# Gate and up projections as Strassen 2x2 block products, with attention as a phase of its own before the feed-forward

## The chip, the cores and the metric

The kernel runs on one core of one Trainium2 chip. The metric is the device time of one execution in microseconds (us). Three runs of the kernel before gave 1727.75, 1727.91 and 1728.28 us. Engines are named as in the profile: PE (matrix products), PEld (its weight loads), DVE (vector), ACT (scalar), POOL, and SP, whose queue issues the DMAs.

## The reference

One input `x` (2048 tokens by 576) goes through two branches which are mixed per token by a sigmoid gate:

```python
g = sigmoid((x * gate_w).sum(-1, keepdims=True))
# a: 32 heads of 18; q, k, v = x @ wqkv; pq = q @ w_phi, pk = k @ w_phi by head
phi = concat(softmax(p), softmax(-p))              # for pq and pk
kv  = phi_k^T v;  z = sum_s phi_k                  # over all tokens
a   = concat_heads(phi_q kv / (phi_q z + 1e-6)) @ wo
# b: gated feed-forward, 4608 hidden
b = (relu(x @ W_gate) * (x @ W_up)) @ W_down
return g * a + (1 - g) * b
```

Everything is float32. The sum over all tokens in `kv` must be finished before any query output can be made; the feed-forward needs nothing of attention.

## The kernel before

Every float32 operand is split into a rounded high part and the exact remainder (`split`: ACT writes `h`, then DVE writes `l = src - h`). A product of two split operands is three matmuls (high by high, low by high, high by low). A contraction of 576 is four tiles of 128 rows and a fifth tile that holds the last 64 rows twice, which needs two matmuls only: `products` yields 4 x 3 + 2 = 14 matmuls for a 128 x 512 result.

Work is tiled by 512 tokens (`TB`, four blocks `tb`) and by 128 hidden rows (36 chunks `c`); `units` holds all 144 pairs.

1. **Keys and values.** For each of 16 token tiles of 128: projections `pk`, `pv` (28 matmuls each of the two), `dual_softmax` (DVE row maxima and minima, two subtractions, ACT exponential, DVE sums, reciprocals) and `scale_heads`, then `kv_step` adds to five PSUM accumulators `kv`.
2. **Feed-forward with attention between its pieces.** For each unit, `gate_up(u, between)` makes the 14 `gate` matmuls, the 14 `up` matmuls, and the hidden rows (times 1 - g, split in `hh`, `hl`); `down(u - 1)` adds 14 matmuls to five PSUM accumulators `acc` that stay open for a whole token block. Between gate and up, `between()` advances the generator `attention(tb)` by one piece: a half projection `pq`, a group of four transposes `ptr`, one `po` product, or one of five output products, which add straight into `acc` (L443). So attention's PE work stands in small pieces between matmuls of the feed-forward, and its DVE and ACT work has a whole token block of 36 units to be done in.

The weights of a unit (928 KB: gate, up and down) are loaded and split again for each of the four token blocks, so 144 times. The order of instructions on each engine is set by a scheduler from the program's order and dependencies; each engine then works through its own list in order.

In the changed kernel (line numbers are its own) the steps that the prediction names are `queries`, `turn` and `outputs` (attention's three parts), `x_operands` and `operand` (the split operands of x), `split_blocks`, `split_sums`, `split_down` (a unit's weights), `product`, `down` and `finish`.

Of the kernel before, what the change touches and what calls it, by code (L numbers as in the profile page):

```python
# [7 lines left out]
F32 = mybir.dt.float32  # L8
# [6 lines left out]
DH = D // H  # L15
# [14 lines left out]
WB = 2 * DK + D  # L30
# [3 lines left out]
def gated_mix_kernel(  # L34
    ctx: ExitStack,
    tc: tile.TileContext,
    xT: bass.AP,
    wqT: bass.AP,
# [4 lines left out]
    wb: bass.AP,  # L43
# [4 lines left out]
    """Products in float32 run as float32r ones: each operand is split exactly into two parts of  # L48
    12 significant bits. A contraction of 576 is four tiles of 128 and a tile that holds the last
    64 rows twice, high parts above low parts."""  # L50
    nc = tc.nc
    PSUM = bass.MemoryType.PSUM

    keep = ctx.enter_context(tc.tile_pool(name="keep", bufs=1))
    raw = ctx.enter_context(tc.tile_pool(name="raw", bufs=2))
    xp = ctx.enter_context(tc.tile_pool(name="xp", bufs=2))
    wp = ctx.enter_context(tc.tile_pool(name="wp", bufs=3))
    hp = ctx.enter_context(tc.tile_pool(name="hp", bufs=2))
    soft = ctx.enter_context(tc.tile_pool(name="soft", bufs=2))
    pp = ctx.enter_context(tc.tile_pool(name="pp", bufs=3, space=PSUM))  # L60

    ident = keep.tile([P, P], F32, name="ident")
    mask = keep.tile([G, G], F32, name="mask")
    ones = keep.tile([1, P], F32, name="ones")
    gs = keep.tile([P, NT], F32, name="gs")
    wq_h = keep.tile([P, 5, D], F32R, name="wq_h")
    wq_l = keep.tile([P, 5, D], F32R, name="wq_l")
# [4 lines left out]
    def split(hi, lo, src):  # L72
        nc.scalar.activation(hi, src, AF.Copy)  # L73
        nc.vector.tensor_tensor(out=lo, in0=src, in1=hi.bitcast(F32), op=ALU.subtract)  # L74
# [8 lines left out]
    def split_x4(x4, src):  # L83
        nc.scalar.activation(x4, src, AF.Copy)
        nc.vector.tensor_tensor(out=x4[64:], in0=src[64:], in1=x4[64:].bitcast(F32), op=ALU.subtract)
# [12 lines left out]
    def products(wh, wl, x, xs=slice(0, TB)):  # L98
        xh, xl, x4 = x
        for k in range(4):  # L100
            yield wh(k), xh[:, k, xs]
            yield wl(k), xh[:, k, xs]
            yield wh(k), xl[:, k, xs]
        yield wh(4), x4[:, xs]
        yield wl(4), x4[:, xs]
# [12 lines left out]
    def dual_softmax(p):  # L118
        """exp(p - max p) and exp(min p - p) by head, and the reciprocals of their sums."""
# [5 lines left out]
        e = soft.tile([P, 2, D], F32, name="e")  # L125
        eh = e.rearrange("p s (h f) -> p s h f", f=DH)
        nc.vector.tensor_tensor(out=eh[:, 0], in0=ph, in1=mx[:, :, None].to_broadcast([P, H, DH]),
                                op=ALU.subtract)
        nc.vector.tensor_tensor(out=eh[:, 1], in0=mn[:, :, None].to_broadcast([P, H, DH]), in1=ph,
                                op=ALU.subtract)  # L130
        nc.scalar.activation(e, e, AF.Exp)
        sm = soft.tile([P, 2 * H], F32, name="sm")
        nc.vector.tensor_reduce(out=sm, in_=e.rearrange("p s (h f) -> p (s h) f", f=DH), axis=AX, op=ALU.add)
# [4 lines left out]
    def scale_heads(e, r):  # L138
        eh = e.rearrange("p s (h f) -> p (s h) f", f=DH)
        nc.vector.tensor_tensor(out=eh, in0=eh, in1=r[:, :, None].to_broadcast([P, 2 * H, DH]), op=ALU.mult)  # L140

# [1 line left out]
    units = [(tb, c) for tb in range(NTB) for c in range(NC)]  # L143
    RAW, W, HID, NGB = {}, {}, {}, {}

    def load_chunk(u):
        if u < len(units):
            RAW[u] = raw.tile([P, WB], F32, name="wbr", tag="raw")
            nc.sync.dma_start(RAW[u], wb[units[u][1]])

    def split_half(u, o):
        if u < len(units):
            h = wp.tile([P, DK], F32R, name="gh")
            l = wp.tile([P, DK], F32R, name="gl")
            split(h, l, RAW[u][:, o:o + DK])
            W[u, o] = h, l

    def split_rest(u):
        if u < len(units):
            split_half(u, DK)  # L160
            w = RAW.pop(u)[:, 2 * DK:]
            dh = wp.tile([P, DK], F32R, name="dh")
            dl = wp.tile([P, 512], F32R, name="dl")
            nc.scalar.activation(dh[:, :D], w, AF.Copy)
            nc.vector.tensor_tensor(out=dl, in0=w[:, :512], in1=dh[:, :512].bitcast(F32), op=ALU.subtract)
            nc.vector.tensor_tensor(out=dh[:, D:], in0=w[:, 512:], in1=dh[:, 512:D].bitcast(F32), op=ALU.subtract)
            W[u] = dh, dl

    def half(u, o, name):
        h, l = W.pop((u, o))  # L170
        ps = bank(name)
        accumulate(ps, products(lambda k: h[:, k * P:(k + 1) * P], lambda k: l[:, k * P:(k + 1) * P],
                                X[units[u][0]]))
        return ps

    def gate_up(u, between=lambda: None):
        """A chunk of hidden rows, times 1 - g. The weights of the next chunks are split meanwhile."""
        r = hp.tile([P, TB], F32, name="r", bufs=1)
        hh = hp.tile([P, TB], F32R, name="hh")
        hl = hp.tile([P, TB], F32R, name="hl")  # L180
        nc.scalar.activation(r, half(u, 0, "gate"), AF.Relu)
        split_rest(u + 1)
        between()
        nc.vector.tensor_tensor(out=r, in0=r, in1=half(u, DK, "up"), op=ALU.mult)  # L184
        nc.vector.tensor_tensor(out=r, in0=r, in1=NGB[units[u][0]], op=ALU.mult)  # L185
        split(hh, hl, r)
        split_half(u + 2, 0)
        HID[u] = hh, hl

    def gates(tb):  # L190
        """1 - g of a block's tokens, on every partition."""
        pg = bank("pg")
        for i in range(4):
            t = 4 * tb + i
            nc.tensor.transpose(pg[:, i * P:(i + 1) * P], gs[:, t:t + 1].to_broadcast([P, P]), ident)  # L195
        NGB[tb] = keep.tile([P, TB], F32, name="ngb", bufs=2)
        nc.scalar.activation(NGB[tb], pg, AF.Copy, bias=1.0, scale=-1.0)

# [12 lines left out]
    with tc.tile_pool(name="ps_v", bufs=1, space=PSUM) as ps_v:  # L211
        pv = [[(bank("pv") if n < 3 else ps_v.tile([P, TB], F32, name=f"pv{n}"))[:, :VC[n % 2][1]]
               for n in (2 * i, 2 * i + 1)] for i in range(4)]
        # TensorE's clock gate opens while the first loads arrive.
        warm = hp.tile([P, TB], F32R, name="hh")
# [82 lines left out]
    load_chunk(0)  # L298
    load_chunk(1)
    split_half(0, 0)  # L300
    split_rest(0)
    load_chunk(2)
    split_half(1, 0)
    fold(wqT, wq_h, wq_l)
    gates(0)
    gate_up(0)
# [3 lines left out]

# [1 line left out]
    a2 = ctx.enter_context(tc.tile_pool(name="a2", bufs=1))  # L312
    pt = ctx.enter_context(tc.tile_pool(name="pt", bufs=22))
    st = ctx.enter_context(tc.tile_pool(name="st", bufs=1))
    kt = [pt.tile([GS, 2, G], F32, name="kt", tag="pt") for _ in range(NG)]
    for j, (c0, gn) in enumerate(GROUPS):
# [234 lines left out]
```

## Time and profile before

| what | value |
|---|---|
| runs | 1727.75, 1727.91, 1728.28 us |
| profiled execution: span of its core | 1724.7 us (the median of the runs is 3.2 us above this span) |
| PE busy / matmuls | 1714.8 us / 8243 |
| DVE busy | 971.1 us |
| ACT busy | 669.2 us |
| granted PE clock | 0.998 on average |
| DMA | 170.33 MB, mean 99 GB/s |

The busy time of an engine is the time in which at least one of its instructions ran, so instructions that overlap their neighbours count once there, while the mean length of one instruction is its full length. Starts of consecutive matmuls are closer than one matmul is long, since they are pipelined. The chain of waits names, from the end backwards, what each step waited for. A few matmul records are missing from the trace.

### The profile page before, as it was taken

What the parts mean: (1) busy time and instruction counts of PE and PEld (TensorE: products, weight loads), DVE (VectorE), ACT (ScalarE), POOL (GpSimd) and SP (SyncE); (2) the same over time, 40 slices, a digit from 0 to 9 for tenths busy, and PEclk for the clock granted to TensorE, in tenths of its full rate; (3) what the DMA queues carried; (4) which work ended last, traced back from release to release, by engine and by line L of the source; (5) the groups of instructions that cost most, each with busy time, mean ns of one, the idle gap of its engine ahead of it and who ended that gap; (6) DMA issues with size and microseconds to landing.
All of it is one profiled execution on the core that took longest, in us unless ns stands there. A gap on an engine that the chain in (4) does not pass through costs nothing.

```text
span 1724.7 us, 20764 instructions
## 1 busy us (share of the span) xinstructions
PE 1714.8 (99%) x8243; PEld 1448.3 (84%) x8243; DVE 971.1 (56%) x1628; ACT 669.2 (39%) x1175; POOL 2.1 (0%) x21
## 2 busy tenths in 40 slices
PE   8999999999999999999999999999999999999998
PEld 8999888888888888888888888888888888888887
DVE  4878576654444667654444666644444756654443
ACT  4344433343333443433333433443333434433322
POOL 0000000000000000000000000000000000000000
PEclk9999999999999999999999999999999999999999
DMA  6102122332332322323332322323232322333311
GB/s 204 32 32 75 67 89 92 105 122 101 108 116 88 110 107 89 119 89 107 109 109 99 116 89 89 119 93 111 101 119 89 116 89 89 121 109 112 102 67 50
DMA packets 36652, 170.33 MB, mean 99 GB/s; under 512 B 3930, under 2 KB 4058, under 8 KB 36556
## 3 DMA queue, kind: packets, MB, share of 16 engines
q1 hardware_dynamic: 36556, 169.02, 28.6%
q8 instruction: 64, 1.05, 0.2%
q14 instruction: 32, 0.26, 0.0%
HBM read 159.04 MB, written 4.72 MB: 95 GB/s over the span
## 4 chain that ended last, share of the span: by engine, by line
PE 98%; DMA 1%; DVE 0%; ACT 0%; issue 0%; SPq 0%; DVEq 0%
PE up L110 27%; PE gate L110 27%; PE acc L458 26%; PE pk L110 3%; PE pq L110 3%; PE acc L443 3%; PE pv L110 3%; PE kv L274 2%; PE po L110 2%; PE ptr L378 1%; PE psf L259 1%; DMA xwv<-wv 1%; DMA xr<-xT 0%; PE pz L330 0%; PE pg L195 0%; PE pz L333 0%
## 5 line engine op out<-in xcount | busy, mean ns | idle before, releaser
L73 ACT ACTIVATE gh<-wbr 128x640 fp32r<-128x640 f32 x288 | 213.6, 742 | 599.1 <-PE gate L110 331.6
L74 DVE TENSOR_TENSOR gl<-wbr,gh 128x640 fp32r<-128x640 f32 x288 | 236.7, 822 | 280.8 <-ACT gh L73 280.8
L458 PE MATMUL acc<-hh,dh 128*128 128x512 f32 x720 | 280.2, 389 | 0.0
L458 PE MATMUL acc<-hl,dh 128*128 128x512 f32 x720 | 280.1, 389 | 0.0
L184 DVE TENSOR_TENSOR r<-r,up 128x512 f32<-128x512 f32 x144 | 99.0, 688 | 246.2 <-PE up L110 245.8
L110 PE MATMUL up<-xh,gh 128*128 128x512 f32 x576 | 229.4, 398 | 0.0
L110 PE MATMUL up<-xh,gl 128*128 128x512 f32 x576 | 225.0, 391 | 0.0
L110 PE MATMUL up<-xl,gh 128*128 128x512 f32 x576 | 224.8, 390 | 0.0
L110 PE MATMUL gate<-xh,gh 128*128 128x512 f32 x576 | 224.3, 389 | 0.0
L110 PE MATMUL gate<-xl,gh 128*128 128x512 f32 x576 | 224.1, 389 | 0.0
L110 PE MATMUL gate<-xh,gl 128*128 128x512 f32 x576 | 224.1, 389 | 0.0
L458 PE MATMUL acc<-hh,dl 128*128 128x512 f32 x576 | 224.1, 389 | 0.0
L73 ACT ACTIVATE hh<-r 128x512 fp32r<-128x512 f32 x144 | 91.1, 633 | 186.4 <-DVE r L185 186.3
L458 PEld LDWEIGHTS acc<-hh,dh 128*128 128x128 f32 x720 | 135.2, 188 | 28.0
L458 PEld LDWEIGHTS acc<-hl,dh 128*128 128x128 f32 x720 | 135.2, 188 | 28.0
L74 DVE TENSOR_TENSOR hl<-r,hh 128x512 fp32r<-128x512 f32 x144 | 99.5, 691 | 78.0 <-ACT hh L73 77.1
L110 PEld LDWEIGHTS up<-xl,gh 128*128 128x128 f32 x576 | 108.1, 188 | 23.4
L110 PEld LDWEIGHTS gate<-xl,gh 128*128 128x128 f32 x576 | 108.1, 188 | 22.5
L458 PEld LDWEIGHTS acc<-hh,dl 128*128 128x128 f32 x576 | 108.1, 188 | 22.5
L110 PEld LDWEIGHTS gate<-xh,gh 128*128 128x128 f32 x576 | 108.1, 188 | 22.5
L110 PEld LDWEIGHTS gate<-xh,gl 128*128 128x128 f32 x576 | 108.1, 188 | 22.4
L110 PEld LDWEIGHTS up<-xh,gh 128*128 128x128 f32 x576 | 108.2, 188 | 20.5
(146 smaller groups left out, 2466.0 us busy)
## 6 DMA issues: line engine op xcount, KB each, us to landing
wbr<-wb SPq DMA_DIRECT2D x144, 928.0 KB
wor<-wo SPq DMA_DIRECT2D x20, 320.0 KB
xr<-xT SPq DMA_DIRECT2D x7, 768.0 KB
outT<-o SPq DMA_DIRECT2D x16, 256.0 KB
xr<-xT SPq DMA_DIRECT2D x7, 512.0 KB
xwv<-wv SPq DMA_DIRECT2D x5, 291.0 KB
xwv<-xT SPq DMA_DIRECT2D x5, 256.0 KB
wr<-wkT SPq DMA_DIRECT2D x2, 630.0 KB
```

Of the source, the lines that this page charges most:

```text
L73: nc.scalar.activation(hi, src, AF.Copy)
L74: nc.vector.tensor_tensor(out=lo, in0=src, in1=hi.bitcast(F32), op=ALU.subtract)
L110: nc.tensor.matmul(ps, w, m, start=i == 0, stop=i == len(pairs) - 1)
L184: nc.vector.tensor_tensor(out=r, in0=r, in1=half(u, DK, "up"), op=ALU.mult)
L259: nc.tensor.matmul(ps[:, d, :gn], w[:gn, j - j0, (d0 + d) * P:(d0 + d + 1) * P], bd[:gn, j, :gn], start=True, stop=True)
L274: nc.tensor.matmul(kv[j][:gn + 1, :, :gn], p[:, D + j * GS:D + j * GS + gn + 1], e[:, :, c0:c0 + gn], start=t == 0, stop=t == NT - 1)
L378: nc.tensor.transpose(ps[:gn, n * P:(n + 1) * P], e[:, s, c0:c0 + gn], ident)
L443: nc.tensor.matmul(acc[m], a, b, start=False, stop=False)
L458: nc.tensor.matmul(acc[m], w, h, start=c == 0 and i == 0, stop=c == NC - 1 and i == len(pairs) - 1)
```

## The change

Three phases now follow each other, with everything of one phase closed before the next one's buffers are opened.

1. **Keys and values**: as before; the feed-forward's first loads, splits and first unit that stood at its end are gone.
2. **Queries and attention's output**, for 16 tiles of 128 tokens (blocks in the order 3, 0, 1, 2): `queries` of tile n, then `turn` of tile n - 2 (ten transposes and splits), and after each block `outputs`, of which a piece is taken after each group of transposes. The output products go to a PSUM bank of their own (`pwo`), are copied by ACT and written by DMA to `att` in DRAM (20 writes).
3. **Feed-forward**, in two halves of 1024 tokens and 36 chunks (72 units). The weights [gate; up] (two row blocks) by the contraction's halves of 288 are one 2x2 block matrix; x by contraction halves and token blocks of 512 the other. Seven block products replace eight. A contraction of 288 is two tiles of 128 and one tile of 32 rows held three times (high, high, low against high, low, high), so a block product is 2 x 3 + 1 = 7 matmuls of 512 columns. Seven sums or blocks of x (`x_operands`) are made and split once per half; four of the weights' (`split_sums`) and three plain blocks (`split_blocks`) once per unit. The results are put together in PSUM (`cx`, `ca`, `cy` accumulate over products) and by three DVE additions. The multiplication by 1 - g moves from the hidden rows to the end (`finish`), where `att` is read back (20 reads) and added. `down` takes two units at a time; two of its ten results stay in PSUM, eight are added to SBUF accumulators by DVE (by ACT in the first group).

The core of the diff:

```diff
-        if u:
-            load_chunk(u + 2)
-            gate_up(u, between)
-            down(u - 1)
...
-            for a, b in pairs:
-                nc.tensor.matmul(acc[m], a, b, start=False, stop=False)
+            ps = pw.tile([P, TB], F32, name="pwo", tag="pw")
+            accumulate(ps, pairs)
...
+                nc.scalar.activation(o, ps, AF.Copy)
...
+            nc.sync.dma_start(att[m * P:m * P + n, ts], o)
...
+    for n in range(len(tiles) + 2):
+        if n < len(tiles):
...
+            queries(tb, i)
+        if n >= 2:
+            for b0 in (0, 4, 8):
+                turn(*tiles[n - 2], b0)
+                if behind:
+                    next(behind, None)
+            if tiles[n - 2][1] == 3:
+                for _ in behind or ():
+                    pass
+                behind = outputs(tiles[n - 2][0])
+    for _ in behind:
+        pass
+    ab.close()
...
+        def operand(name, a):
+            o = xo.tile([P, 5, TB], F32R, name="xo", tag="xo")
+            nc.scalar.activation(o[:, 0:3], a, AF.Copy)
+            tt(out=o[:, 3:5], in0=a[:, 0:2], in1=o[:, 0:2].bitcast(F32), op=SUB)
+            tt(out=o[32:64, 2], in0=a[32:64, 2], in1=o[32:64, 2].bitcast(F32), op=SUB)
+            XO[hf, name] = o
...
+    def split_w(o, a, n):
+        nc.scalar.activation(o[:, :, 0:3], a, AF.Copy)
+        tt(out=o[:, :, 3:5], in0=a[:, :, 0:2], in1=o[:, :, 0:2].bitcast(F32), op=SUB)
+        tt(out=o[64:96, :, 2], in0=a[64:96, :, 2], in1=o[64:96, :, 2].bitcast(F32), op=SUB)
...
+            tt(out=s[:, 0], in0=a[:, 2], in1=a[:, 3], op=ADD)
+            tt(out=s[:, 2], in0=a[:, 0], in1=a[:, 3], op=SUB)
+            tt(out=s[:, 1], in0=s[:, 0], in1=a[:, 0], op=SUB)
+            tt(out=s[:, 3], in0=a[:, 1], in1=s[:, 1], op=SUB)
...
+    def product(ps, u, n, first):
+        o, i = WO[u][n]
+        x = XO[units[u][0], n]
+        pairs = [(o[:96, i, 2], x[:96, 2])]
+        for k in range(2):
+            pairs += [(o[:, i, k], x[:, k]), (o[:, i, 3 + k], x[:, k]), (o[:, i, k], x[:, 3 + k])]
+        for m, (w, v) in enumerate(pairs):
+            nc.tensor.matmul(ps, w, v, start=first and m == 0, stop=m == len(pairs) - 1, skip_group_check=True)
...
+        tt(out=o, in0=a, in1=ngb[:n, ts], op=MULT)
+        tt(out=o, in0=o, in1=g, op=ADD)
+        nc.sync.dma_start(out[m * P:m * P + n, ts], o)
...
+            if not perm:
+                if g == 0:
+                    ACC[m, t] = ac.tile([P, TB], F32, name=f"ac{m}{t}")
+                    nc.scalar.activation(ACC[m, t], ps, AF.Copy)
                 else:
-                    nc.vector.tensor_tensor(out=o, in0=b, in1=acc[m][:64], op=ALU.add)
+                    tt(out=ACC[m, t], in0=ps, in1=ACC[m, t], op=ADD)
+            if g == NGR - 1:
+                finish(hf, m, t, ACC.pop((m, t)))
```

**Where instructions stand.** First PE, in the middle of the first token block of the kernel before (`ptr` is a group of attention's transposes):

```order
L110 MATMUL gate<-xl,gh 128x512
L110 MATMUL gate<-x_1364,gh 128x512
L110 MATMUL gate<-x_1364,gl 128x512
L378 MATMUL ptr<-ident,e 126x128 x4
L110 MATMUL up<-xh,gh 128x512
L110 MATMUL up<-xh,gl 128x512
```

and PE of the changed kernel where attention ends and the feed-forward begins (`cx`, `ca`, `cy` are PSUM results of block products):

```order
L124 MATMUL pwo<-oh,woh 128x512
L124 MATMUL pwo<-ol,woh 128x512
L522 MATMUL cx<-xo,wb 128x512 x7
L522 MATMUL ca<-xo,ws 128x512 x7
L522 MATMUL cx<-xo,wb 128x512 x7
L522 MATMUL cx<-xo,ws 128x512 x14
L522 MATMUL cy<-xo,wb 128x512 x7
```

Before, attention's piece stands between a gate and an up product; now no block product stands ahead of attention's last `pwo`.

Second, DVE within a tile of queries. Before:

```order
L123 TENSOR_REDUCE mx<-pq 128x32
L124 TENSOR_REDUCE mn<-pq 128x32
L127 TENSOR_TENSOR e<-pq,mx 128x576
L129 TENSOR_TENSOR e<-mn,pq 128x576
L184 TENSOR_TENSOR r<-r,up 128x512
L74 TENSOR_TENSOR gl<-wbr,gh 128x640
L185 TENSOR_TENSOR r<-r,ngb 128x512
L133 TENSOR_REDUCE sm<-e 128x64
L74 TENSOR_TENSOR hl<-r,hh 128x512
```

and in the changed kernel, where operations of two tiles and the splits `phTl` of a third stand between each other:

```order
L312 TENSOR_TENSOR v_2347<-v_2347,r_2345 128x64
L137 TENSOR_REDUCE mx_2489<-pq_2456 128x32
L314 SCALAR_TENSOR_TENSOR den_2355<-v_2347 128x32
L88 TENSOR_TENSOR phTl_2378<-ptr_2360,phTh_2377 126x128
L315 RECIPROCAL den_2355<-den_2355 128x32
L138 TENSOR_REDUCE mn_2490<-pq_2456 128x32
L317 SCALAR_TENSOR_TENSOR r_2345<-r_2345,gs_80,den_2355 128x64
L88 TENSOR_TENSOR phTl_2398<-ptr_2392,phTh_2397 126x128
L152 TENSOR_TENSOR e_2339<-e_2339,r_2345 128x1152
```

The feed-forward's operations that stood between those of attention (`r`, `gl`, `hl`) are gone from this stretch.

Third, DVE of the changed kernel where the second half's operands of x are made (`xo` low parts, `xr` differences of x blocks), between the additions of running units (`ac`, `u2`, `g1`):

```order
L447 TENSOR_TENSOR xo_8688<-xr_8684,xo_8688 128x1024
L448 TENSOR_TENSOR xo_8688<-xr_8684,xo_8688 32x512
L454 TENSOR_TENSOR xr_8684<-xr_8686,xr_8684 128x1536
L461 TENSOR_TENSOR xr_8686<-xr_8726,xr_8686 128x1536
L447 TENSOR_TENSOR xo_8703<-xr_8684,xo_8703 128x1024
L448 TENSOR_TENSOR xo_8703<-xr_8684,xo_8703 32x512
L572 TENSOR_TENSOR ac01_4631<-pd_8744,ac01_4631 128x512
L458 TENSOR_TENSOR xr_8684<-xr_8726,xr_8684 128x1536
L613 TENSOR_TENSOR u2_8707<-cx_8676,u2_8707 128x512
L618 TENSOR_TENSOR g1_8692<-cy_8767,g1_8692 128x512
```

Nothing like these rows stood in the kernel before: it split x as loaded, with no differences.

486 lines of the change are left out of this document (292 added, 194 removed).

## The prediction

> **What bounds the kernel now.** I read the page's busy shares, then the chain that ended last (summed by line, then its last pieces), then the waits.
>
> ```profile
> PE 1714.8 (99%) x8243; PEld 1448.3 (84%) x8243; DVE 971.1 (56%) x1628; ACT 669.2 (39%) x1175; POOL 2.1 (0%) x21
> ```
> ```profile
> by line: PE up L110 26.7%; PE gate L110 26.5%; PE acc L458 26.5%; PE pk L110 3.4%; PE pq L110 3.4%; PE acc L443 3.4%; PE pv L110 2.6%; PE kv L274 1.7%; PE po L110 1.6%; PE ptr L378 1.0%; PE psf L259 0.6%; DMA xwv<-wv 0.5%; DMA xr<-xT 0.4%;
> ```
> ```profile
> 1648.18 3.17 PE up L110 x14
> ...
> 1713.69 6.36 PE acc L458 x28
> ```
> ```profile
> DVE r L184 <- PE up L110: 245.8, 116, 6.7
> ```
>
> PE is never idle after the first 25 us, and DVE waits for it, not the other way round. So time is the sum of matmul starts: 3.17/14 = 0.2266 us for one of 512 columns. The three feed-forward rows take 79.7% of 1724.7 us = 1375 us for 6048 matmuls; everything else 350 us. Of that, attention's queries (`pq` 3.4, L443 3.4, `po` 1.6, `ptr` 1.0%) are 9.4% = 162 us. The last matmul ends at 1720.05, 4.65 us ahead of the end. The forecast is made against the span of 1724.7; the median of the runs lies 3.2 us above it.
>
> **What it removes.** Gate and up go from 144 x 28 = 4032 matmuls to 72 x 49 = 3528; `down` keeps 2016. 504 x 0.2266 = **-114.2 us**, all of it on the path, since PE is the bound. The order confirms these counts, so that the change doesn't do what it says is excluded.
>
> **What it adds: attention loses its cover.** The 162 us of PE work stay, but DVE's part of it, formerly under 36 units of feed-forward for each block, now has only that PE work beside it. DVE per tile of 128 queries:
>
> ```profile
> L123 DVE TENSOR_REDUCE mx<-pq 128x32 f32<-128x576 f32 x16 | 12.0, 753 | 15.3 <-ACT pq L350 15.3
> L124 DVE TENSOR_REDUCE mn<-pq 128x32 f32<-128x576 f32 x16 | 11.9, 743 | 0.0
> L127 DVE TENSOR_TENSOR e<-pq,mx 128x576 f32<-128x576 f32 x16 | 12.0, 749 | 0.0
> L129 DVE TENSOR_TENSOR e<-mn,pq 128x576 f32<-128x576 f32 x16 | 12.0, 752 | 0.0
> L133 DVE TENSOR_REDUCE sm<-e 128x64 f32<-128x1152 f32 x32 | 43.2, 1350 | 10.7 <-ACT e L131 10.6
> L135 DVE RECIPROCAL r<-sm 128x64 f32<-128x64 f32 x32 | 17.5, 548 | 0.2
> L359 DVE TENSOR_TENSOR u<-e,zb 128x576 f32<-128x576 f32 x32 | 22.8, 754 | 0.0
> L360 DVE TENSOR_REDUCE v<-u 128x32 f32<-128x576 f32 x32 | 23.9, 748 | 0.0
> L362 DVE TENSOR_TENSOR v<-v,r 128x64 f32<-128x64 f32 x16 | 3.5, 220 | 0.1
> L364 DVE SCALAR_TENSOR_TENSOR den<-v 128x32 f32<-128x32 f32 x16 | 3.1, 192 | 0.5
> L365 DVE RECIPROCAL den<-den 128x32 f32<-128x32 f32 x16 | 5.6, 348 | 0.3
> L367 DVE SCALAR_TENSOR_TENSOR r<-r,gs,den 128x64 f32<-128x64 f32 x16 | 4.4, 278 | 0.1
> L140 DVE TENSOR_TENSOR e<-e,r 128x1152 f32<-128x1152 f32 x32 | 43.2, 1349 | 0.2
> L74 DVE TENSOR_TENSOR phTl<-ptr,phTh 126x128 fp32r<-126x128 f32 x128 | 36.7, 287 | 21.4 <-ACT phTh L73 20.7
> ```
>
> With u and v twice and ten `phTl` the lengths add to 13.2 us a tile, 211 us for 16. Two loads of x (three splits each) and the output splits of the blocks that fall before the last `phTl` add 26 us by the rows below: 237 us. But a length isn't a period:
>
> ```profile
> 205.28 0.74 DVE L124 TENSOR_REDUCE mn<-pq 128x32 f32<-128x576 f32 x1
> 205.94 0.75 DVE L127 TENSOR_TENSOR e<-pq,mx 128x576 f32<-128x576 f32 x1
> ...
> 216.10 0.19 DVE L364 SCALAR_TENSOR_TENSOR den<-v 128x32 f32<-128x32 f32 x1
> 216.32 0.35 DVE L365 RECIPROCAL den<-den 128x32 f32<-128x32 f32 x1
> ```
>
> Independent neighbours start 0.08 us before the one ahead ends; dependent ones start 0.03 after. The stretch has some 425 operations, so it lasts 237 - 425 x 0.08 = 203 us at least; I take 0.05, since the new order puts independent operations between each other: 216. Waits come on top. The split of a transposed block goes ACT, DVE, ACT, DVE on one PSUM bank, and the sums wait for the exponential. By the rows above the first kind of wait cost 20.7 us for 128 splits (26 for 160), the second 10.6 for 32 sums (5 for the 16 of the queries). Bounds: 0, if other operations cover them all, to 31; I take 20, near the upper end, because 48 output matmuls in a row (11 us) stand ahead of transposes in the new PE order. DVE's stretch: **236 us (203 to 268)**, more than PE's 162: DVE becomes the bound of this phase.
>
> It starts when the first `pq` is copied:
>
> ```profile
> 174.51 0.64 PE L274 MATMUL kv<-e,kvp 128*127 128x252 f32 x2
> ```
> ```profile
> 185.98 0.62 PE pz L330 x2
> 186.60 0.37 PE pz L333 x2
> ...
> 188.94 1.84 PE pq L110 x14
> ```
> ```profile
> L350 ACT ACTIVATE pq<-pq 128x288 f32<-128x288 f32 x32 | 13.2, 412 | 27.3 <-PE pq L110 27.3
> L73 ACT ACTIVATE hh<-r 128x512 fp32r<-128x512 f32 x144 | 91.1, 633 | 186.4 <-DVE r L185 186.3
> ```
>
> `kv` ends near 175.1, five setups of 0.99 take 5, two half projections 3.7, the copy 0.4, with hand-overs 184.8. Attention's DVE stretch ends at 421. Then the last block's outputs run alone, since nothing of the feed-forward is ahead of them on PE: the rest of the 53 `pwo` matmuls of the block before (5 us past the last split), 30 `po` (6.8), copy, DMA and split of the last rows (6.2, with the DMA row below), 49 `pwo` (11.1), then copy 0.6, the DMA to `att` 4, and 1.5 for the weights' first split, whose buffer waits for those writes: 35 us. First block product at **456**. PE's feed-forward used to have 350 us outside itself in the whole kernel; now 456 stand before its first product: **+106 us**.
>
> ```profile
> 1.17 3.65 DMA xwv<-wv
> ```
>
> **The feed-forward's steady state** costs nothing beyond its matmuls if DVE keeps up: 77 x 0.2266 = 17.45 us a unit. DVE lengths by these rows (0.158 us + 1.041 ns a column):
>
> ```profile
> L184 DVE TENSOR_TENSOR r<-r,up 128x512 f32<-128x512 f32 x144 | 99.0, 688 | 246.2 <-PE up L110 245.8
> L74 DVE TENSOR_TENSOR hl<-r,hh 128x512 fp32r<-128x512 f32 x144 | 99.5, 691 | 78.0 <-ACT hh L73 77.1
> L74 DVE TENSOR_TENSOR gl<-wbr,gh 128x640 fp32r<-128x640 f32 x288 | 236.7, 822 | 280.8 <-ACT gh L73 280.8
> L74 DVE TENSOR_TENSOR xl<-xr,xh 128x1536 fp32r<-128x1536 f32 x7 | 12.3, 1757 | 7.4 <-ACT xh L73 7.3
> L166 DVE TENSOR_TENSOR dh<-wbr,dh 128x64 fp32r<-128x64 f32 x144 | 31.4, 218 | 0.0
> ```
>
> Blocks 0.96 + 0.56, four weight sums 2.23, their splits 1.22 + 0.69, down weights 0.91, three additions 2.06, two products 1.38, two `hl` 1.38, four accumulations 2.76: 14.2 us, 12.9 with the overlap. The tightest wait is for ACT's rounding between a product's result and its low part, a few tenths. I take 0, with 12.9 us under 17.45; the other end is in the rivals. ACT has two copies of 1152 and 1536 columns, one of 576, five of 512, some 6.5 us.
>
> **Its three edges** are not covered. (a) Start: the seven operands of x cost DVE four differences of 1.76 and seven splits of 1.22 + 0.69 = 20.4 us; two operands are made under attention's tail. DVE needs some 31 us to the first unit's last operand, in which PE finds 9 products (14.3 us): **+17** (10 to 25, by how much of the second unit goes ahead). (b) Change of halves: another 20.4 beside two units' 28.4, against PE's 34.9, and 14.5 of `finish`: **+14** (5 to 25). (c) End: after the last product 3 us to its low part, some 30 operations of `finish` 19 us, DMA 4, together 26, of which PE's 56 `down` matmuls are 12.7; 4.65 were there before: **+9** (4 to 13).
>
> Loads fall from 144 of 928 KB to 72 of 768 + 288 KB and the 40 `att` transfers are 10 MB: no wait, at 99 GB/s before. SP's queue gets some 80 issues more, spread over the whole span; in the attention phase only `wo` loads stand behind them, ahead of need.
>
> **Sum:** 1724.7 - 114.2 + 106 + 17 + 14 + 9 = 1756.5 span; + 3.2 = **1760 us**.
>
> **Rivals.** *Tight packing, faster.* Saving and losses are near each other: if every DVE neighbour overlaps and nothing waits (203 instead of 236) and the edges cost 10, 6 and 5, the span is 1724.7 - 114.2 + 73 + 21 = 1704.5, time **1708**. It decides if attention's DVE stretch is 32 us shorter than I say. For it: 0.0 idle in most rows above. Against: the two wait rows, and the long `pwo` run.
>
> *PE at half clock in attention.* A gap of 3.08 us near the start is followed by half clock:
>
> ```profile
> 24.33 7.23 PE L259 MATMUL psf<-bd,wr 126*128 126x126 f32 x38 [3.08 <-ACT kvp L245]
> ```
> ```profile
> 24.00:30.00 6.00, 5.67 (x26) 5.70 (x27) 1.71 (x4) 3.01 (x12) 0.38 (x4) 0.50 0.54 179
> 30.00:33.00 3.00, 2.71 (x23) 2.49 (x22) 1.70 (x5) 1.63 (x4) 0.00 (x0) 0.98 0.35 105
> ```
>
> (The third number from the end is the granted clock.) In attention each tile's 13 us of DVE hold 5 us of PE work without outputs (28 `pq`, ten transposes) and 10 with them (162/16), so PE idles 3 to 8 us a tile. If the clock stayed at 0.50 throughout, 162 would be 324 and PE the bound: 180.6 + 324 + 12 of hand-overs = 517 instead of 456, time **1821**. Against: 5.8 us of dense work brought full clock back at 30, and half-clocked work is dense. [...]
>
> *DVE too slow in the feed-forward.* In-order waits of DVE for ACT or PE eat the 4.5 us of room, and each unit gets 1 us longer: 72 more, **1832**. For it: 280.8 us of `gl` waiting for ACT; against: that wait was behind PE, and the new order keeps ACT's part well ahead.
>
> **How the numbers follow.** Forecast 0.58, own range 1735 to 1790; packing 0.12; half clock 0.15; slow DVE 0.15. The range takes 1720 to 1825: it cuts most of packing and half of the last. 0.2% is 3.5 us, about what a measurement tells from no change. Faster 0.11 (nearly all of packing), same 0.05 (between packing and forecast), slower 0.84.
>
> **What would show it.** In the profile after: PE idle and DVE at 85% or more from 185 to 421; first `cx` near 456; then PE over 95% but for some 15 us at the start, 15 around the middle of what is left, and the end; matmuls 0.2266 us apart there. Wrong if DVE in attention is under 80% busy (then a wait, not its work, sets the phase), if the clock there is 0.5 throughout, or if PE has gaps in each unit.

## The result, and the profile after

| what | before | changed kernel |
|---|---|---|
| median of the runs | 1727.84 us (1727.75 to 1728.28, 4 runs) | 1804.64 us (1804.34 to 1806.09, 4 runs) |
| ratio | | 1.0449, 95% interval 1.0435 to 1.0464 |
| profiled execution's span | 1724.7 us | 1802.7 us |
| PE matmuls / busy | 8243 / 1714.8 us | 7739 / 1672.5 us |
| DVE busy | 971.1 us | 1347.0 us |

The change makes the kernel 76.8 us slower. The forecast was 32 us slower (1760): the direction was right, and so was the phase in which most of the loss arises, but the forecast loss was less than half of the measured one. The measured time lies inside the range (1720 to 1825) and outside the forecast's own one (1735 to 1790).

First the page of the changed kernel: busy times, three rows of the 40 slices (45 us each), and the chain that ended last by engine.

```profile
PE 1672.5 (93%) x7739; PEld 1390.9 (77%) x7739; DVE 1347.0 (75%) x2193; ACT 657.3 (36%) x1062; POOL 2.1 (0%) x21
...
PE   8999668876589999999999999899999999999996
...
DVE  4976898982586787777777777997777767777765
...
PEclk9999878878789999999999999999999999999998
...
PE 82%; DVE 9%; DMA 5%; ACT 2%; issue 1%; SPq 0%; DVEq 0%; ACTq 0%
```

Before, PE was nearly the whole chain:

```profile
PE 98%; DMA 1%; DVE 0%; ACT 0%; issue 0%; SPq 0%; DVEq 0%
```

Now it is 82%, and the holes lie together: slices 5 to 12 (180 to 540 us) hold attention's phase, its tail and the feed-forward's start; then PE is full but for slice 26 (1127 to 1172 us, the change of halves) and the end. The windows show who is full where. Columns: us of the window, busy us of PE, PEld, DVE, ACT, POOL with their instructions, granted PE clock, DMA share, GB/s.

```profile
200.00:250.00 50.00, 30.21 (x161) 27.09 (x161) 48.05 (x101) 18.50 (x53) 0.00 (x0) 0.78 0.09 27
250.00:300.00 50.00, 34.43 (x160) 28.42 (x161) 45.76 (x99) 23.30 (x61) 0.00 (x0) 0.80 0.19 53
300.00:350.00 50.00, 43.51 (x239) 36.87 (x237) 44.90 (x96) 23.85 (x63) 0.00 (x0) 0.91 0.23 67
350.00:400.00 50.00, 38.86 (x172) 30.73 (x172) 43.39 (x96) 23.68 (x62) 0.00 (x0) 0.77 0.27 84
...
420.00:440.00 20.00, 16.68 (x71) 12.48 (x69) 4.69 (x7) 7.96 (x14) 0.00 (x0) 1.00 0.59 168
440.00:460.00 20.00, 7.38 (x16) 4.64 (x16) 8.62 (x11) 5.98 (x8) 0.00 (x0) 0.59 0.47 141
460.00:480.00 20.00, 12.81 (x49) 10.18 (x49) 5.64 (x9) 7.58 (x10) 0.00 (x0) 0.84 0.24 79
```
```profile
600.00:700.00 100.00, 100.00 (x438) 82.17 (x437) 73.71 (x119) 31.73 (x44) 0.00 (x0) 1.00 0.20 65
```

From 200 to 400 us DVE is busy 182.1 of 200 and PE 147.0: this phase is DVE's, as predicted. From 420 to 480 no engine is full: this is the tail, a chain of single steps. From 600 to 700 us, in the steady part, PE is busy all the time at full clock.

The tail, by the timeline of ACT and PE (start, length, engine, line, operation; in brackets the idle time before it and what ended it; between these rows other work is left out):

```profile
430.66 0.60 ACT L350 ACTIVATE og<-po 126x512 f32<-126x512 f32 x1 [0.16 <-PE po L124]
432.33 0.60 ACT L350 ACTIVATE og<-po 126x512 f32<-126x512 f32 x1 [1.07 <-PE po L124]
434.82 0.63 ACT L87 ACTIVATE oh<-or 128x512 fp32r<-128x512 f32 x1 [1.89 <-DMA or<-og]
435.35 0.58 ACT L350 ACTIVATE og<-po 126x512 f32<-126x512 f32 x1
...
439.65 0.63 ACT L87 ACTIVATE oh<-or 128x512 fp32r<-128x512 f32 x1 [3.72 <-DMA or<-og]
440.19 0.58 ACT L350 ACTIVATE og<-po 126x512 f32<-126x512 f32 x1
...
448.38 0.63 ACT L87 ACTIVATE oh<-or 128x512 fp32r<-128x512 f32 x1 [7.61 <-DMA or<-og]
448.91 0.58 ACT L350 ACTIVATE og<-po 72x512 f32<-72x512 f32 x1
...
457.42 1.48 ACT L446 ACTIVATE xo<-xr 128x1536 fp32r<-128x1536 f32 x1 [5.18 <-DVE xr L454]
458.81 0.61 ACT L98 ACTIVATE oh<-or 128x512 fp32r<-128x512 f32 x1
...
460.94 0.79 PE L124 MATMUL pwo<-oh,woh 128*128 128x512 f32 x1 [6.57 <-DVE oh L99]
...
477.51 1.16 ACT L481 ACTIVATE wb<-wr 128x1152 fp32r<-128x1152 f32 x1 [3.13 <-DMA att<-o]
...
480.43 3.32 PE L522 MATMUL cx<-xo,wb 96*128 96x512 f32 x7 [6.69 <-DVE wb L483]
```

This is a ladder. `outputs` copies a group (og), moves its rows by DMA (or), splits full rows (oh), and only then copies the next group. In ACT's list the later copies stand behind splits that wait for a DMA, 1.9, 3.7 and 7.6 us, although their `po` is ready: the last group's last `po` starts at 437.22 and takes 0.40 us, and its copy starts at 448.91. The last split (L98) even stands behind an operand of x for the next phase. The last 49 output products start at 460.94, and the first block product at 480.43.

### The profile page after: what moved, and what is told of

Same layout as the page of the kernel before. It is cut to its first block, busy times and chain, and to the rows that moved or that the text cites. A ratio compares the mean times of both kernels' runs of the same rounds, so it can differ in the third digit from the quotient of the medians.

```text
span 1802.7 us, 20128 instructions
## 1 busy us (share of the span) xinstructions
PE 1672.5 (93%) x7739; PEld 1390.9 (77%) x7739; DVE 1347.0 (75%) x2193; ACT 657.3 (36%) x1062; POOL 2.1 (0%) x21
## 4 chain that ended last, share of the span: by engine, by line
PE 82%; DVE 9%; DMA 5%; ACT 2%; issue 1%; SPq 0%; DVEq 0%; ACTq 0%
PE cx L522 25%; PE pd L565 19%; PE ca L522 12%; PE cy L522 6%; PE pm L565 5%; PE pk L124 3%; PE pwo L124 3%; PE pv L124 3%; PE kv L229 2%; PE pq L124 2%; DMA or<-og 1%; PE po L124 1%; DMA xr<-xs 1%; DVE v L310 1%; DMA ga<-att 1%
## 5 line engine op out<-in xcount | busy, mean ns | idle before, releaser
L565 PE MATMUL pd<-hh,wd 128*128 128x512 f32 x1008 | 357.8, 391 | 2.1 <-DVE ac L572 2.1
L522 PE MATMUL cx<-xo,wb 128*128 128x512 f32 (+1 forms) x1008 | 259.7, 398 | 12.0 <-DVE wb L483 8.5
L522 PE MATMUL cx<-xo,ws 128*128 128x512 f32 (+1 forms) x1008 | 258.8, 396 | 6.4 <-DVE xo L448 4.6
L522 PE MATMUL ca<-xo,ws 128*128 128x512 f32 (+1 forms) x1008 | 258.5, 396 | 2.2 <-DVE ws L483 2.2
L572 DVE TENSOR_TENSOR ac<-pd,ac 128x512 f32<-128x512 f32 x272 | 187.4, 689 | 70.1 <-PE pd L565 68.1
L522 PEld LDWEIGHTS cx<-xo,wb 128*128 128x128 f32 (+1 forms) x1008 | 192.3, 191 | 56.1 <-ACT ws L481 7.1
L522 PEld LDWEIGHTS cx<-xo,ws 128*128 128x128 f32 (+1 forms) x1008 | 191.4, 190 | 51.5 <-issue 5.3
L522 PEld LDWEIGHTS ca<-xo,ws 128*128 128x128 f32 (+1 forms) x1008 | 191.7, 190 | 45.7 <-ACT wb L481 2.6
L565 PE MATMUL pd<-hl,wd 128*128 128x512 f32 x576 | 224.4, 390 | 0.0
L565 PEld LDWEIGHTS pd<-hh,wd 128*128 128x128 f32 x1008 | 189.8, 188 | 42.9 <-DVE ac L572 3.5
```

What stands on the lines that cost most here:

```text
L522: nc.tensor.matmul(ps, w, v, start=first and m == 0, stop=m == len(pairs) - 1, skip_group_check=True)
L565: nc.tensor.matmul(ps, w, v, start=i == 0 and (g == 0 or not perm), stop=i == len(pairs) - 1 and (g == NGR - 1 or not perm))
L572: tt(out=ACC[m, t], in0=ps, in1=ACC[m, t], op=ADD)
```

## The experiments

Times are medians. The kernel before stood at 1725.6 to 1727.9 in the groups of runs, so a difference of 2 us between groups is not read as a difference of kernels.

### What each half of the change costs

Two kernels without attention's queries and outputs: the changed kernel, and the one before.

```diff
# changed kernel
-    for n in range(len(tiles) + 2):
-        ... queries, turn, outputs
+    for tb in range(NTB):
+        gates(tb)
...
-        tt(out=o, in0=o, in1=g, op=ADD)      # att, in finish
# kernel before: attention(tb) yields without work, gates stay
```

> The changed kernel without attention's second phase: queries, transposes and outputs are left out, and the end does not read or add `att` (the output lacks attention). Keys and values, the gates and the whole feed-forward stay. By my account the first block product comes near 190 instead of 480 us and nothing else changes but some us at the two `finish` stages: 1510 to 1518. To be compared with the kernel before without the same part: mine says the feed-forward alone is 40 to 55 us faster in the new form. Rival, that the new form of the feed-forward gains nothing (its DVE work takes the gain back): 1555 or more.

> The kernel before without attention's pieces between its matmuls: queries, transposes, outputs and their setup are left out (the output lacks attention); the gates stay. If they cost only their PE time there, 162 us and 5 of setup go: 1556 to 1562. If in the kernel before they also cost waits, less is left: under 1550.

Measured: 1498.67 us (changed, 1495.96 to 1500.63) and 1554.85 us (before, 1553.79 to 1557.10). The rows of the first one that matter are its first block product and the last matmul:

```profile
187.61 3.20 PE L501 MATMUL cx<-xo,wb 96*128 96x512 f32 x7 [9.71 <-DMA wdr<-wd]
...
1490.41 0.39 PE L541 MATMUL pd<-hl,wd 128*128 128x512 f32 x1
```

So the feed-forward alone gains 56.2 us in the new form. Attention costs 1727.9 - 1554.9 = 173 us in the kernel before and 1804.6 - 1498.7 = 306 us in the changed one: 133 us more. -56 + 133 = +77 is the whole result; it adds up by construction, and the two sizes are what the runs tell. The new form of the feed-forward gains, its starts and ends included; the phases in order cost more than twice its gain. The time without attention came out 11 us under what I expected for the changed kernel (and 1 us under for the kernel before), so attention's price in the changed kernel is higher than I had it.

### Does the seven-product form save its PE time?

```diff
-    seven products per unit, operands = sums of blocks (x: 7, weights: 4 sums + 3 blocks)
+    eight products per unit, operands = plain blocks (x: 4, weights: 4)
```

> The same phases and tiles, but gate and up as eight plain block products instead of seven (four blocks of x and four of the weights, split as they are; no sums, no differences, one copy of the gate product by ACT and one multiplication for each hidden tile). PE gets 504 matmuls back: 504 x 0.2306 = 116 us; the operands of x take 3 splits and 4 differences fewer, 8 to 15 us less at the start and the change of halves. Theory that the seven-product form does save its PE time: 1895 to 1915. Rival, that DVE's added work takes back most of the saving: under 1860.

Measured 1889.86 us (1886.24 to 1892.02), 5 us under the expected range and far from the rival's 1860: the seven-product form saves 85 us in these phases. First block product and last matmul of this kernel:

```profile
485.15 5.31 PE L491 MATMUL cx<-xo,wb 96*128 96x512 f32 x12 [7.37 <-DVE wb L465]
...
1874.41 0.40 PE L534 MATMUL pd<-hl,wd 128*128 128x512 f32 x1
```

Between them lie 1389.7 us; 72 units of 56 x 0.2306 + 28 x 0.2266 = 19.26 us are 1386.7. So with eight plain products the two edges (start, change of halves) cost 3 us. In the changed kernel they cost 36: from 480.43 to 1786.67 are 1306.2 us, and 72 units of 17.64 are 1270.1. The 116 us of matmuls saved are real; 33 of them go to the two edges, which are that much longer with the sums, differences and extra splits of the seven-product form. I had expected 8 to 15 there in this run, although the prediction's own edge terms (17 + 14) were near.

### Is a matmul of 96 rows dearer?

The steady unit was 17.64 us instead of 17.45. In the changed kernel, two starts of the same product a unit apart:

```profile
599.34 1.78 PE L522 MATMUL ca<-xo,ws 96*128 96x512 f32 x7
...
616.98 1.78 PE L522 MATMUL ca<-xo,ws 96*128 96x512 f32 x7
```

```diff
-        pairs = [(o[:96, i, 2], x[:96, 2])]
+        pairs = [(o[:, i, 2], x[:, 2])]
```

> Each block product's first matmul uses 128 rows (the last 32 are zeros in both operands) instead of 96; nothing else changes. In the changed kernel's steady state the seven matmuls of a product start 0.2306 us apart, those of `down` 0.2266. Theory that the mix of a 96-row matmul with 128-row ones costs this: 504 x 7 matmuls x 0.004 = 14 us less, about 1791. Rival, the spacing belongs to where the operands lie or to something else: 1804 to 1805, spacing still 0.2306.

Measured 1793.77 us (1791.65 to 1799.98), 10.9 less. The same pair of rows in this kernel:

```profile
1002.40 1.75 PE L522 MATMUL cx<-xo,wb 128*128 128x512 f32 x7
...
1019.85 1.75 PE L522 MATMUL cx<-xo,wb 128*128 128x512 f32 x7
```

17.45 us a unit, as predicted for matmuls of 0.2266. With one matmul of 96 rows among six of 128, the seven starts are 0.004 us further apart on average. They are not so evenly: from 600 to 1000 us the first four steps of such a product are 0.2324, 0.2376, 0.2324 and 0.2308 us, the other three 0.2267, which makes 0.027 us a product. Of the 13.7 us that come back in the units, some 3 went to the edges: from the first block product to the last matmul this kernel's profile has 39 us beyond its 72 units, the changed kernel's 36. Why the edges grew isn't shown.

### Does DVE set attention's phase?

```diff
# e5: once more the same
             tt(out=u, in0=e[:, s], in1=zb[:, s], op=MULT)
+            tt(out=u, in0=e[:, s], in1=zb[:, s], op=MULT)
# e7: on POOL
-            tt(out=u, in0=e[:, s], in1=zb[:, s], op=MULT)
+            nc.gpsimd.tensor_tensor(out=u, in0=e[:, s], in1=zb[:, s], op=MULT)
```

> Each of the 32 multiplications `u` of the queries is done twice on DVE (the same result is written again). If DVE's own work sets the pace of attention's phase, as predicted, 32 x 0.75 less 32 x 0.08 of overlap = 21 to 24 us more: 1826 to 1829. If PE at a lower granted clock, or waits between ACT and DVE, set it, the doubled work fits in gaps: less than 6 us more, under 1811.

> The 32 multiplications `u` of the queries run on POOL instead of DVE; nothing is left out. If DVE's own work sets attention's phase and POOL can take its share beside it, up to 32 x 0.70 = 22 us less: 1782 to 1792. If POOL and DVE hinder each other, or if the chain through `u` becomes longer and that sets the pace: 1804 or more.

Measured: 1823.33 us doubled (18.7 more), 1785.03 us on POOL (19.6 less). 32 operations cost or give back 0.58 to 0.61 us each, of a length of 0.745. Doubling cost 2 us less than the expected 21 to 24, but three times what the rival allowed, and the move to POOL lies in its range: DVE sets this phase for the most part. In the changed kernel PE's granted clock there was 0.77 to 0.91 (the windows above), and from 200 to 204 us, behind 4.52 us of idle PE, 0.50; but the time followed DVE's work both ways, so the clock didn't set it. On POOL the same product is twice as long, off the path:

```profile
L309 POOL TENSOR_TENSOR u<-e,zb 128x576 f32<-128x576 f32 x32 | 48.1, 1523 | 163.3 <-ACT e L143 163.3
```

### What makes the tail long?

First the ladder alone: all groups are copied and moved, then split.

```diff
             nc.scalar.activation(g[:gn], po[:gn], AF.Copy)
             for k in range(5): ... dma or <- og
-                    if b == min((k + 1) * P, D): split(oh, ol, R[k])
             yield
+        for k in range(5): split(oh, ol, R[k])
```

> In `outputs` all five groups' matmuls, copies and transfers come first, and the splits of the gathered rows (oh, ol) follow in a loop of their own; nothing is left out. My theory is that in attention's tail each split ahead of the next group's copy in ACT's order makes the next copy wait for a DMA round trip (429 to 461 us in the changed kernel's profile, 31.7 us where I had predicted 13): the first block product then comes 13 to 19 us earlier and the time is 1785 to 1792. Rival, that the transfers are late because the next phase's loads stand ahead of them on the same queue: the copies come early but the splits still end near 461, time within 3 us of 1804.6.

Measured 1795.34 us (1791.77 to 1796.66), 9.3 less: between the two answers. ACT in this kernel:

```profile
431.45 0.60 ACT L350 ACTIVATE og<-po 126x512 f32<-126x512 f32 x1
...
436.99 0.59 ACT L350 ACTIVATE og<-po 72x512 f32<-72x512 f32 x1 [0.79 <-PE po L124]
...
442.09 5.62 SPq L441 DMA_DIRECT2D xr<-xs  x2
447.66 0.63 ACT L87 ACTIVATE oh<-or 128x512 fp32r<-128x512 f32 x1 [5.92 <-DMA or<-og]
...
450.04 0.69 DVE L99 TENSOR_TENSOR oh<-or,oh 64x512 fp32r<-64x512 f32 x1
```

The five copies now take 6 us instead of 19 and the last split ends 10 us earlier. The ladder is gone, but gathered rows still come late, with the next phase's loads right behind them on the one queue. So both theories may have a part; how much of this wait is the loads' isn't shown. That the tail isn't shorter by more has another reason: the block before's run of output products now stands ahead of the last transposes on PE, so attention's last split ends at 433.4 instead of 416.9.

Next the buffers, the slots, and wide splits (`turn` splits a group of four transposes at once; `po` is made for all groups ahead of the next tile).

```diff
# e9: order of pools            # e6
-    xo, raw6, wop              -    tp = ... bufs=5
+    raw6, wop, xo              +    tp = ... bufs=9
# e10
-            split(h[:gn, ts], l[:gn, ts], ps[:gn, n * P:(n + 1) * P])      # four times
+        split(h[:gn, :, ts], l[:gn, :, ts], ps[:gn, ...])                  # once for four blocks
...
+                next(behind)          # all five po at once; splits of oh two pieces later
```

> The pool that holds the feed-forward's temporary tiles and those of `finish` has nine slots instead of five. If the end of the changed kernel (19.9 us after the last matmul, 13.3 predicted) is long because the loads of `att` wait for slots that the output transfers free, the end shrinks by 5 to 8 us, and the change of halves, which runs the same code, by 0 to 5: 1792 to 1800. If the end is only DVE's work and the last transfer, 1804 to 1805.

> The feed-forward's buffers are laid out in another order: those of the first loads and weight splits (raw6, wop) come first, where attention's queries (done some 80 us before the first block product) had theirs, and the seven operands of x after them; nothing else changes. If the hand-over between the phases (6.7 us of idle PE before the first `cx`, for the weights' split) and a part of the slow start behind it (operands of x, made only after attention's last matmul) come from buffers that attention's output still holds: 8 to 18 us less, 1787 to 1797. If the order of DVE's and ACT's lists sets them, not the buffers: 1802 to 1807.

> In the queries, the splits of a group of four transposes are one instruction on ACT and one on DVE (128 x 4 columns) instead of four; the five `po` products of a block, their copies and transfers come in one piece, ahead of the next tile, and the splits of the gathered rows two pieces later; nothing is left out. Attention's DVE work falls by 4 x 0.29 - 0.69 twice and 2 x 0.29 - 0.42 once a tile, 1.1 us or 17 us in 16 tiles; of the tail's 64 us between the last split and the first block product the ladder's 18.7 and the late output run's 8 should go. Theory (DVE's work and a serial tail set the time to the first product): 30 to 44 us less, 1761 to 1775. If only the tail counts: 1778 to 1790; if neither, 1800 or more.

Measured: e6 1801.15 us (3.5 less, between its two answers), e9 1798.56 us (6.1 less, under the 8 to 18 expected), e10 1774.86 us (29.8 less, at the edge of the 30 to 44). The 19.9 us that e6's expectation names are 16.0 by the trace: the last matmul ends at 1786.67 of 1802.7. In e10 the first block product came at 453.04 instead of 480.43, which is 27 of the 30 us. e9 shows why the order of pools gave little:

```profile
472.88 1.48 ACT L446 ACTIVATE xo<-xr 128x1536 fp32r<-128x1536 f32 x1 [3.20 <-DMA att<-o]
```

In the changed kernel the weights' split waited 3.13 us for attention's last output (477.51 above); here the first operand of x waits 3.20 for it. The wait had changed its owner, and the first block product came at 476.52 instead of 480.43.

### Putting it together, until both kernels are beaten

f2 takes the padded rows, `u` on POOL, wide splits, e9's pools, and the differences of x on POOL.

> The edits that go with the theory together: 128-row matmuls in every product, `u` on POOL, wide splits with `po` ahead, the other order of buffers, and the four differences of x blocks (twice) on POOL; nothing is left out. The sum of the measured single gains (11 for the rows, 20 for `u`) and the expected ones (30 to 44, 8 to 18, and 4 to 10 for the differences at the two edges), less some overlap between them: 65 to 95 us below the changed kernel, 1710 to 1740. So it may or may not beat the kernel before (1727.9); above 1750 the gains overlap far more than I think.

Measured 1765.32 us, 39 less than the changed kernel instead of 65 to 95. The single gains measured before (11, 20, 30 and 6) make 66, so either they overlap or something in f2 costs time. ACT in its tail:

```profile
406.98 1.06 ACT L353 ACTIVATE og<-po 126x512 f32<-126x512 f32 x2
...
415.79 1.16 ACT L487 ACTIVATE wb<-wr 128x1152 fp32r<-128x1152 f32 x1 [7.76 <-DMA wr<-wgu]
416.86 0.57 ACT L353 ACTIVATE og<-po 72x512 f32<-72x512 f32 x1
...
445.49 1.48 ACT L452 ACTIVATE xo<-xr 128x1536 fp32r<-128x1536 f32 x1 [3.20 <-DMA att<-o]
```

Work of the next phase had moved into the tail, but to a bad place: a weight split stands ahead of attention's last copy and waits for its load. And the first operand of x still waits for attention's last write. f4 changes both: the second unit's load comes before those of x, and the buffers of the last output tiles lie behind all that the feed-forward opens with.

```diff
-    pt = ...; (ph4 behind it)
+    ph4 = ...; pt = ...
-    raw6 = ... bufs=4
+    raw6 = ... bufs=5
     load_w(0)
+    load_w(1)
```

> As f2, but the buffers that hold attention's last output tiles lie above those of the feed-forward's first loads, weight splits and all operands of x (ph4 ahead of pt, five raw6 slots, the second unit's load first), so that none of these waits for attention's last transfers. In f2's profile the first split of an operand of x waits 3.2 us for the last write to `att` and PE stands 7.5 us, and a weight split stands ahead of the last copy of `po` on ACT (8.8 us of idle PE). If the place of the buffers is what keeps the feed-forward out of attention's tail: block products stand between `po` and `pwo` on PE, and the operands of x are made there too; the tail's idle PE (some 20 us from 402 to 449) and about half of the slow start (some 10 of 18 us) go: 25 to 35 us less than f2, 1730 to 1740. If the tail is bound by ACT, DVE or the transfers' own time instead: less than 10 less, above 1755.

> As f4, with half of each query tile's scaling (the second 576 columns of `e`) on POOL instead of DVE and six slots for the temporaries instead of five. If DVE still sets attention's stretch, 16 x 0.65 = 10 us less there, and 1 to 2 at the end: 8 to 12 less than f4. If the stretch is by now set by PE's runs of output products and the waits between engines (DVE was 84% busy in f2 from 200 to 400), 0 to 4 less.

Measured: f4 1741.50 us, 23.8 less than f2 and just short of the expected 25 to 35; its first block product starts at 412.53, ahead of attention's last output products. f5 1733.72 us (7.8 less, just short of its 8 to 12 and well over the 0 to 4 of the other answer): DVE still set most of the stretch, though f5 also has one slot more for temporaries.

f6 puts the differences of x back on DVE; f7 also issues the gathering transfers of every second row tile from POOL's queue.

```diff
-        nc.gpsimd.tensor_tensor(out=b11, in0=b12, in1=b11, op=SUB)     # and three more
+        tt(out=b11, in0=b12, in1=b11, op=SUB)
...
-                    nc.sync.dma_start(R[k][...], g[...])
+                    (nc.gpsimd if k % 2 else nc.sync).dma_start(R[k][...], g[...])
```

> As f5, with the differences of x blocks on DVE again (1.76 us each there, 3.5 to 4.3 on POOL in f2's profile). In f5's profile ACT waits 14.4 and 13.0 us for these POOL differences at the two edges and PE loses 8 of the 30 us from 1060 to 1090. If their length on POOL sets the edges: 4 to 8 us less than f5, 1726 to 1730, level with the kernel before. If DVE is the bound there anyway: 1732 to 1737.

> As f6, with the transfers that gather the rows of every second tile of attention's output issued from POOL's queue instead of SP's. In f5's profile PE stands 8.6 us in the tail for the first gathered rows, and each issue takes some 0.9 us on SP, ten in a row with the loads of weights and x between them. If the issue queue sets that wait: 4 to 9 less than f6, 1718 to 1726, below the kernel before. If the transfers themselves, or the loads beside them, set it: within 3 of f6.

Measured, five runs each: f6 1717.41 us (1717.02 to 1720.43), ratio to the kernel before 0.9955 (0.9941 to 0.9968); f7 1714.27 us (1711.27 to 1716.24), ratio 0.9930 (0.9918 to 0.9942). Both beat the kernel before, by 0.45% and 0.7%. f7 lies 3 us under f6: close to the lower answer, so the queue was a small part of that wait. f6 gave 14 to 16 us, twice what I expected. From the first block product to the last matmul f5 takes 1313.0 us and f6 1297.5, so nearly all of it lies there, where the differences are. Rows of f2 and of f5 show POOL's difference of x and the DVE operations that ran beside it. First f2:

```profile
449.14 3.47 POOL L460 TENSOR_TENSOR xr<-xr 128x1536 f32<-128x1536 f32 x1 [64.01 <-DVE xo L454]
...
452.69 3.78 POOL L467 TENSOR_TENSOR xr<-xr 128x1536 f32<-128x1536 f32 x1
```
```profile
449.68 3.48 DVE L517 TENSOR_TENSOR wd<-wdr,wd 128x512 fp32r<-128x512 f32 x1 [0.76 <-ACT wd L516]
453.09 3.46 DVE L518 TENSOR_TENSOR wd<-wdr,wd 128x64 fp32r<-128x64 f32 x1
```

Then f5:

```profile
1070.01 4.32 POOL L477 TENSOR_TENSOR xr<-xr 128x1536 f32<-128x1536 f32 x1 [7.58 <-DVE xo L456]
1071.05 3.83 DVE L456 TENSOR_TENSOR xo<-xr,xo 32x512 fp32r<-32x512 f32 x1
```

The DVE operations of these three rows take 0.69, 0.22 and 0.68 us elsewhere. Here each ends only after POOL's operation has ended. So a difference on POOL took its own 3.47 to 4.32 us in these rows, against DVE's 1.76, and DVE's time too. In f5 the eight differences took 29.5 us instead of 14.1, and five DVE operations beside them 13 us more than alone; how the gain divides between the two isn't shown. In f5 and in f6, the window where the change of halves begins:

```profile
1050.00:1080.00 30.00, 21.40 (x77) 15.98 (x76) 22.20 (x22) 12.83 (x13) 14.76 (x4) 0.79 0.11 36
```
```profile
1050.00:1080.00 30.00, 27.69 (x114) 20.29 (x112) 29.75 (x44) 12.63 (x15) 0.00 (x0) 1.00 0.29 89
```

PE starts 114 matmuls in these 30 us instead of 77. And this is what cover looks like in f7, by PE's timeline in the tail:

```profile
403.11 0.47 PE L530 MATMUL cx<-xo,wb 128*128 128x512 f32 x1 [4.16 <-ACT oh L87]
...
410.46 0.80 PE L124 MATMUL pwo<-oh,woh 128*128 128x512 f32 x1 [3.41 <-ACT oh L87]
...
414.84 1.55 PE L530 MATMUL cx<-xo,wb 128*128 128x512 f32 x6
...
428.51 1.77 PE L530 MATMUL ca<-xo,ws 128*128 128x512 f32 x7
```

Block products stand between attention's last output products, and right behind these, at 428.51, the next one follows without a gap. In the changed kernel 6.7 us of idle PE stood there, 52 us later.

## Why the prediction was wrong

The forecast's span was 1756.5; the profile after has 1802.7. By its own steps:

| step | predicted | measured | difference |
|---|---|---|---|
| matmuls removed | 504 | 504 (8243 to 7739) | 0 |
| attention's DVE stretch ends | 421 | 416.9 | -4 |
| tail to the first block product | 35 | 63.5 | +28 |
| steady unit, 72 of them | 17.45 us | 17.64 us | +14 |
| start and change of halves | 17 + 14 | 36 | +5 |
| last matmul to the end | 13.3 | 16.0 | +3 |

The differences add to +46, which is the miss.

**The step that failed** is the tail: "35 us" between attention's last split and the first block product. It was a sum of lengths along one path: 5 for the rest of the block before's output products, 13 for `po`, copy, DMA and split, 11 for the last products, 6 for the hand-over. Measured were 12.3, 31.7, 12.8 and 6.7. The first was off because the last of these products needs a split that stood behind the last transposed block, so the whole last run began only when the stretch was over (417.83). The second was off because I took the five groups as parallel, with one DMA at the end. In ACT's list they stand in a row, each copy behind a split that waits for the DMA of the copy before, and the queue of these DMAs also carried the next phase's loads, which I had put down as "no wait". The third was 1.7 us over, behind 6.57 us of idle PE, with a granted clock of 0.84 from 460 to 480. e2 shows the ladder itself, e9, f2 and f4 the buffers and the order behind it: with the tail covered, the first product of f4 starts at 412.5.

**The steady state** was said to cost nothing beyond 0.2266 us a matmul. I had taken that spacing from matmuls of 128 rows and given it to products with one of 96 rows. e1 settles it: with 128 rows the unit is 17.45. This is a term that was mis-sized, 13.7 us. DVE did keep up, as I had said: PE was busy 100.00 of 100 us from 600 to 700. The rival of a DVE too slow there is refuted.

**Right** were the bound (DVE), since e5 and e7 move the time by 0.6 us for each operation, both ways, and the end of attention's stretch to 4 us. The latter was partly luck. The stretch lasted 230 us (186.83 to 416.86) instead of 236, but DVE was busy 202 of them where I had 216, about what the full overlap of 0.08 us would give, and idle 28 where I had 20 us of waits. The two errors had opposite signs. The rival of half clock in attention got the symptom (clock down to 0.77 over 50 us) but not the effect, since PE wasn't the bound there. Tight packing needed a stretch 32 us shorter than forecast; it was 4 shorter.

**The edges** came out 5 us longer than the 31 predicted. e8 shows that they belong to the sums of blocks and the splits that come with them: with plain blocks 3 us are left.

**The end** is 3 us longer: after the last matmul the additions of `att` wait for loads, which in part need slots of temporaries that the output transfers free.

```profile
1793.08 0.69 DVE L543 TENSOR_TENSOR o<-o,ga 128x512 f32<-128x512 f32 x1 [0.72 <-DMA ga<-att]
...
1796.67 0.69 DVE L543 TENSOR_TENSOR o<-o,ga 128x512 f32<-128x512 f32 x1 [2.89 <-DMA ga<-att]
```

Nine slots (e6) gave 3.5 us in all, while these waits fell from 4.3 to 2.3 us.

What stays open: how much of f2's shortfall belongs to the weight split ahead of the last copy and how much to the DVE operations that took longer beside POOL's differences, since f4 changed several things and f6 undid both the long differences and the long DVE operations; how the late gathered rows in the tail divide between the issue queue and the loads beside them; and what the 5 us at the edges are made of one by one.

## What to carry to other kernels

When work that was hidden under the bound engine becomes a phase of its own, price it twice: by the fullest engine of the phase, and by its tail as a list in each engine's order, where copies, transfers and splits wait for the one ahead (here 1.9, 3.7 and 7.6 us), with the next phase's loads on the same queue. Two things shortened this tail by like amounts: all copies ahead of the splits, in fewer and wider steps (e10, 29.8 us, part of it in the stretch before), and letting the next phase in (f4, 23.8 us). For the second, the next phase's first buffers must not lie where the last outputs still are, and its first instructions must not stand ahead of the tail's own. A saving of 6% of the matmuls was worth 56 us here, and it paid only after a good part of the lost cover (133 us) had been taken back.

## What the runs showed of the hardware

- **One matmul of 96 rows slows its neighbours.** In the changed kernel, seven matmuls of which the first has 96 rows start 0.2306 us apart on average; in e1, with 128 rows in all of them, 0.2266. The delay lies in the first four steps (0.2324, 0.2376, 0.2324 and 0.2308 us, against 0.2267 in the other three). Taking in 32 rows of zeros made the kernel 10.9 us faster. The 0.004 us for each of the seven are 14 us over 3528 matmuls.
- **Some DVE operations took longer beside POOL.** In f2 a DVE operation with two inputs in SBUF took 3.46 us instead of 0.22 beside a POOL operation of 3.78 us, while reductions (one input) in e7, which has `u` on POOL, kept their length (`v` 0.739 us on average, 0.724 in the changed kernel). Additions with one input in PSUM kept theirs too: in f2 three of them (`u2`, `g1`, `ac`; 1087.74 to 1089.62) took 0.68 to 0.69 us each, beside a difference on POOL that ran from 1087.85 to 1091.35. So the differences of 1.76 us each were moved off DVE to a place where, in f5, five of the eight held DVE up for 1.8 to 3.3 us.
